# Transposing K with a permutation, so that the score matmuls read runs of 32 columns in place of a stride of 4

## Chip, cores, metric

One core of one Trainium2 chip. The metric is the device time of one execution in microseconds (us). (A run is classed slow when it lies over 1.5% above the fastest of its kernel.) The engines: PE does the matmuls, ACT and DVE the copies, POOL small preparations, SP issues the DMA loads. PSUM is the memory that PE writes to. The granted clock is the share of PE's full clock that the profile shows as allowed.

## The reference, cut

Two independent attention decodes of one token each, A and B, then a concatenation of their outputs.

```python
# for each of A (last 2048 positions) and B (all 8192 positions); Hq = 32 heads, Hkv = 16, Dh = 128
q = (x @ wq).reshape(B, Sq, Hq, Dh)...          # x is 1 x 576
scores = einsum("bhqd,bhkd->bhqk", q, k) * Dh ** -0.5
o = einsum("bhqk,bhkd->bhqd", softmax(scores), v)
out = o.reshape(B, Sq, Hq * Dh) @ wo             # 576 wide
```

There is one query row per head, so almost nothing is computed per byte: 102.9 MB are read in a run, nearly all of it K, V, wq and wo.

## The kernel before

K and V come in slots of 4 MB, two slots each. The work runs in five stages (`g`), each with two K slots. A load into a slot waits until PE has finished reading what lies in it. All big loads go through one queue, in a fixed order.

In a K slot, one 128x128 block holds 32 positions of four heads: partition `4*x + g` holds position `x` of head `g`. PE transposes each block (identity as the moving matrix), ACT and DVE copy the result from PSUM to `kt`, and the score matmuls read `kt` as moving operand, one head at a time:

```python
def k_transpose(c, u, place):            # a unit: a quarter of a slot, 32 blocks
    for q in range(4):
        for t in range(8):
            pe.matmul(ktps_bf[q][:, t*128:(t+1)*128], lhsT=kslots[s][:, o:o+128],
                      rhs=ident[:, :], start=True, stop=True, is_transpose=True)
        # ... ACT (q even) or DVE (q odd) copies the 128 x 1024 bank to kt

def k_scores(c, a, place):               # 16 matmuls for two units
    for g in range(NG):                  # NG = 4 heads
        for j in range(4):               # four column tiles of the array, 32 columns each
            rhs = kt[:, o:o + 2048].rearrange("d (x g) -> d x g", g=NG)[:, :, g]   # stride 4
            pe.matmul(sacc[32*j:32*j+32, 512*h:512*h+512], lhsT=qst[:, o2:o2+32], rhs=rhs, ...)

# order of loads, by stage; k = half a stage's K, v = a V slot, w = wo
order = ["k0 k1 v0", "k2 k3 v1", "k4 k5 v2", "k6 k7 v3", "k8 k9 v4 v5", "w0 v6 v7", "v8 v9 w1 ..."]
# one stage on PE: transposes of units 0..3 (frees slot 0), scores 0, units 4,5, scores 1,
#   units 6,7 (frees slot 1), scores 2, scores 3; after odd stages the softmax transposes; then V slots
```

(Names and offsets shortened, the rest left out.)

## Time and profile before

| | before |
|---|---|
| median of 4 runs | 259.35 us (259.0 to 259.8) |
| profiled run: time, span | 260.13 us, 258.1 us |
| data read, mean rate over the span | 102.9 MB, 399 GB/s |
| PE busy | 185.7 us |
| score matmuls: busy, one | 38.9 us, 628 ns |

Lines of the page of the kernel before. "GB/s" is what DMA moved in each fortieth of the span. A group's line reads: source line, engine, operation, output from inputs, sizes, count, busy us, mean ns of one, idle time before it.

```profile
span 258.1 us, 7455 instructions
...
GB/s 286 446 403 420 427 427 432 422 465 414 422 420 437 434 442 424 361 253 325 366 366 467 427 406 457 437 330 442 432 401 259 406 442 452 406 416 437 426 405 115
...
L481 PE MATMUL ktps<-ident,kv 128*128 128x128 bf16 x1280 | 81.3, 227 | 14.1 <-PEq L214 13.2
...
L506 PE MATMUL sacc<-kt,qst 128*32 128x512 bf16 x320 | 38.9, 628 | 0.0
```

The GB/s row says that DMA is near 430 nearly everywhere, and that it falls to 253 in the eighteenth slice and 259 in the thirty-first. The stretches give the size of those dips. Columns: window, its length, busy time and count of each engine, mean PE clock, DMA share, GB/s (the last number is the one to read).

```profile
103.00:134.00 31.00, 27.71 (x446) 20.87 (x436) 13.15 (x20) 16.47 (x20) 0.80 (x2) 0.93 0.86 342
134.00:160.00 26.00, 22.46 (x300) 15.07 (x301) 14.48 (x22) 15.00 (x17) 0.81 (x2) 1.00 1.01 435
160.00:190.00 30.00, 27.18 (x556) 21.57 (x560) 14.72 (x23) 14.92 (x16) 0.00 (x0) 0.89 0.97 407
190.00:200.00 10.00, 7.57 (x292) 4.97 (x286) 2.92 (x6) 1.26 (x3) 0.00 (x0) 1.00 0.80 319
```

Against the 435 GB/s of 134 to 160 us, the three other stretches lost 31 x (1 - 342/435) = 6.6 us, 1.9 us and 2.7 us of DMA time. Who caused it is in the timeline of the DMA queue (start, duration, what; consecutive issues merged):

```profile
116.27 11.83 SPq L388 DMA_DIRECT2D kv<-in_B_k_cache_dram  x2
128.14 0.60 SPq L388 DMA_DIRECT2D kv<-in_B_v_cache_dram  x1
...
167.39 3.23 SPq L388 DMA_DIRECT2D kv<-in_B_v_cache_dram  x2
...
195.04 27.37 SPq L388 DMA_DIRECT2D kv<-in_B_v_cache_dram  x4
```

The load at 116.27 us is the first K load of the fourth stage; it could not be issued until the last transpose of the slot it overwrites. And PE was late, as the prediction argues, because it spends long on scores. The same timeline for PE; "x4" are the four column tiles of one group, "x16" four groups. The duration is that of the merged records, which overlap, so take the difference of two starts. In brackets, where there was a wait, stand its length and what ended it; PEq is PE's own sequencer, waiting on a semaphore:

```profile
26.17 0.40 PE L439 MATMUL misc<-kv,xpad 128*32 128x512 bf16 x4
26.39 0.40 PE L439 MATMUL opsum<-kv,xpad 128*32 128x512 bf16 x4
...
116.17 1.99 PE L506 MATMUL sacc<-kt,qst 128*32 128x512 bf16 x16
118.09 3.79 PE L481 MATMUL ktps<-ident,kv 128*128 128x128 bf16 x64
```

A group of four q-projection matmuls (128x32 by 128x512, unit stride) starts every 0.215 us. Sixteen score matmuls, the same size, take 118.09 - 116.17 = 1.92 us, 0.45 us for each group of four once 0.1 us for start and end is taken off.

### The profile page before, as it was taken

The numbers are of one execution on the slowest core, as the hardware profiler recorded it, in microseconds if no ns is written. First come the engines' busy times: TensorE is split into PE (matmuls) and PEld (weight loads), VectorE is DVE, ScalarE is ACT, GpSimd is POOL, SyncE is SP. The second block draws the span as 40 slices with busy tenths as digits, with TensorE's granted clock in tenths as the row PEclk, the third lists the DMA queues.
The fourth block names the chain that finished last, engine by engine and source line by source line (L and its number), as shares of the span: only waits on it lengthen the run. The fifth ranks groups of instructions, "written<-read, shape, count | busy, mean of one in ns | idle before, by whom it ended". The sixth has DMA issues, their size and how long they took to land. (4 is left out here: it accounts for less than half of the span.)

```text
span 258.1 us, 7455 instructions
## 1 busy us (share of the span) xinstructions
PE 185.7 (72%) x3371; PEld 134.3 (52%) x3374; DVE 93.6 (36%) x174; ACT 82.8 (32%) x94; POOL 14.5 (6%) x40
## 2 busy tenths in 40 slices
PE   0047539897799967699969995799996551557654
PEld 0013239572777517596648661587755151447642
DVE  0001315544564481165437446245443800230300
ACT  2000017662676500196549550047741000000000
POOL 8801000000000000000000000000000000000000
PEclk9999957999799975799999999599999755556875
DMA  7999999999999999858989999989996999999993
GB/s 286 446 403 420 427 427 432 422 465 414 422 420 437 434 442 424 361 253 325 366 366 467 427 406 457 437 330 442 432 401 259 406 442 452 406 416 437 426 405 115
DMA packets 5355, 102.92 MB, mean 399 GB/s; under 512 B 864, under 2 KB 992, under 8 KB 1376
## 3 DMA queue, kind: packets, MB, share of 16 engines
q1 hardware_dynamic: 5056, 102.77, 94.3%
q8 instruction: 8, 0.13, 0.2%
q10 hardware_dynamic: 288, 0.00, 0.1%
q14 instruction: 3, 0.02, 0.0%
HBM read 102.76 MB, written 0.00 MB: 398 GB/s over the span
## 5 line engine op out<-in xcount | busy, mean ns | idle before, releaser
L489 ACT ACTIVATE kt<-ktps 128x1024 bf16<-128x1024 bf16 x80 | 75.9, 1028 | 71.5 <-PE ktps L481 71.5
L481 PEld LDWEIGHTS ktps<-ident,kv 128*128 128x128 bf16 x1280 | 78.1, 102 | 25.9 <-issue 25.6
L481 PE MATMUL ktps<-ident,kv 128*128 128x128 bf16 x1280 | 81.3, 227 | 14.1 <-PEq L214 13.2
L492 DVE COPY kt<-ktps 128x1024 bf16<-128x1024 bf16 x80 | 55.2, 691 | 48.9 <-PE ktps L481 48.8
L571 PE MATMUL opsum<-kv,ptm 128*32 128x128 bf16 x1280 | 29.4, 273 | 16.5 <-PEq L214 14.7
L506 PE MATMUL sacc<-kt,qst 128*32 128x512 bf16 x320 | 38.9, 628 | 0.0
L571 PEld LDWEIGHTS opsum<-kv,ptm 128*32 128x32 bf16 x1280 | 27.3, 126 | 20.0 <-issue 20.0
L439 PE MATMUL opsum<-kv,xpad 128*32 128x512 bf16 x72 | 8.9, 471 | 17.2 <-DVE xpad L424 17.2
L506 PEld LDWEIGHTS sacc<-kt,qst 128*32 128x32 bf16 x320 | 8.3, 107 | 17.6 <-issue 16.1
L579 DVE TENSOR_SCALAR acc<-opsum,rows 128x128 f32<-128x128 f32 x5 | 1.8, 351 | 41.9 <-PE opsum L571 41.9
L439 PEld LDWEIGHTS opsum<-kv,xpad 128*32 128x32 bf16 x72 | 2.6, 115 | 19.8 <-issue 18.9
L471 POOL COPY qst<-qtm 128x256 bf16<-128x256 bf16 x10 | 4.0, 402 | 140.0 <-PE sacc L506 127.8
L612 ACT ACTIVATE stat<-stat 128x1 f32<-128x1 f32 (+1 forms) x2 | 0.6, 294 | 32.8 <-DVE stat L610 32.8
L655 PE MATMUL ktps<-kv,opj 128*32 128x144 bf16 x200 | 6.7, 296 | 4.0 <-DMA kv<-in_B_wo_dram 3.5
L554 PE MATMUL misc<-pt,spread 128*128 128x512 bf16 x12 | 5.9, 490 | 5.0 <-PEq L214 3.3
L561 DVE TENSOR_TENSOR ptm<-opsum,hmask 128x512 bf16<-128x512 f32 x12 | 8.3, 691 | 1.8 <-PE misc L545 1.8
L445 ACT ACTIVATE qrow<-opsum 128x512 bf16<-128x512 f32 x2 | 1.2, 598 | 24.1 <-PE misc L439 24.1
L439 PE MATMUL misc<-kv,xpad 128*32 128x512 bf16 x72 | 8.8, 464 | 0.0
L561 DVE TENSOR_TENSOR ptm<-misc,hmask 128x512 bf16<-128x512 f32 x12 | 8.2, 686 | 0.5
L532 ACT ACTIVATE psb<-sacc,stat 128x1024 bf16<-128x1024 f32 x3 | 3.3, 1115 | 15.1 <-DVE stat L530 15.1
L655 PEld LDWEIGHTS ktps<-kv,opj 128*32 128x32 bf16 x200 | 4.9, 128 | 5.7 <-DMA kv<-in_B_wo_dram 5.2
L554 PEld LDWEIGHTS opsum<-pt,spread 128*128 128x128 bf16 x12 | 1.2, 98 | 9.6 <-DVE ptm L561 6.6
(67 smaller groups left out, 63.5 us busy)
## 6 DMA issues: line engine op xcount, KB each, us to landing
kv<-in_B_k_cache_dram SPq DMA_DIRECT2D x8, 4096.0 KB
kv<-in_B_v_cache_dram SPq DMA_DIRECT2D x8, 4096.0 KB
kv<-in_A_k_cache_dram SPq DMA_DIRECT2D x4, 2048.0 KB
kv<-in_A_v_cache_dram SPq DMA_DIRECT2D x4, 2048.0 KB
kv<-in_A_wq_dram SPq DMA_DIRECT2D x1, 4608.0 KB, 13.7
kv<-in_A_wo_dram SPq DMA_DIRECT2D x1, 2592.0 KB, 21.0
kv<-in_B_wq_dram SPq DMA_DIRECT2D x1, 2560.0 KB, 19.4
kv<-in_B_wq_dram SPq DMA_DIRECT2D x1, 2048.0 KB, 23.8
```

The lines of the kernel that those rows point to most:

```text
L439: ins = pe.matmul(qps[c][32 * j:32 * j + 32, :], lhsT=xpad[:, P, x, :], rhs=src[:, o:o + 512], start=(u == 0), stop=(u == WQ_UNITS - 1))
L471: add("pool", lambda pool: pool.tensor_copy(qst[:, s * 256:(s + 1) * 256], qtm[:, o:o + 256]), reads=[("qtm", KIND[g])], writes=[("qst", s ...
L481: ins = pe.matmul(ktps_bf[q][:, t * 128:(t + 1) * 128], lhsT=kslots[s][:, o:o + 128], rhs=ident[:, :], start=True, stop=True, is_transpose ...
L489: add("act", lambda act, q=q, dst=dst: act.activation(dst, ktps_bf[q], ACT.Copy), reads=[("bank", q)], writes=[("kt", u % NKT, q)], tag="e ...
L492: add("dve", lambda dve, q=q, dst=dst: dve.tensor_copy(dst, ktps_bf[q]), reads=[("bank", q)], writes=[("kt", u % NKT, q)], tag="e%d%d" % ( ...
L506: ins = pe.matmul(sacc[32 * j:32 * j + 32, 512 * h:512 * h + 512], lhsT=qst[:, o:o + 32], rhs=rhs, start=False, stop=True, skip_group_chec ...
L532: add("act", lambda act: act.activation(psb[:, :], sacc[:, :], ACT.Exp, bias=st(P, C_NB + k), scale=SCALE, accum_out=st(P, C_L + k)), read ...
L554: add("pe", lambda pe, h=h, i=i, dst=dst: pe.matmul(dst[:, :], lhsT=spread[:, i, :], rhs=pt0[:, h * 512:(h + 1) * 512], start=True, stop=T ...
L561: return dve.tensor_tensor(to, dst[:, :].rearrange("p (f n y) -> p f n y", f=4, n=4), m, ALU.mult)
L571: ins = pe.matmul(opsum[32 * j:32 * j + 32, s * DH:(s + 1) * DH], lhsT=ptm[:, o:o + 32], rhs=vslots[s][:, b * 128:(b + 1) * 128], start=(m ...
L579: add("dve", lambda dve: dve.tensor_scalar(acc[:, g, :], opsum[:, 0:DH], rows[:, KIND[g], 0:1], None, ALU.mult), reads=[B_O, "rows"], writ ...
L655: ins = pe.matmul(ktps[P][32 * j:32 * j + 32, 0:OUTW], lhsT=opj[:, P, jj:jj + 32], rhs=view[:, o:o + OUTW], start=(jj == 0), stop=(jj == H ...
```

## The change

The intent: let the transpose, which is a matmul anyway, put the columns into the order that the scores want. Moving a permutation matrix through in place of the identity sends row `4*x + g` to column `32*g + x`. Each head's 32 columns of a block then lie together, and the scores read runs of 32 elements, 256 bytes apart. Number and size of all matmuls and copies stay.

```diff
+    order = nc.alloc_sbuf_tensor("order", [128, 128], BF16)
 ...
-        for t in (ident, xpad, selq, ...):  pool.memset(t[:], 0.0)
+        for t in (ident, order, xpad, selq, ...):  pool.memset(t[:], 0.0)
 ...
+    add("pool", select(order[:].rearrange("p (g x) -> p g x", g=NG), 0, [[-1, NG], [-4, 32]], 1),
+        reads=["order"], writes=["order"])
 ...
-                                    rhs=ident[:, :], start=True, stop=True, is_transpose=True)
+                                    rhs=order[:, :], start=True, stop=True, is_transpose=True)
 ...
-                    rhs = kt[:, o:o + 2048].rearrange("d (x g) -> d x g", g=NG)[:, :, g]
+                    rhs = kt[:, o:o + 2048].rearrange("d (t g x) -> d t g x", g=NG, x=32)[:, :, g, :]
```

(The list of load names is renamed from `order` to `LOADS`, and dependencies name the new tensor.)

More of the change, by code (lines that the diff above doesn't have):

```diff
@@ L356, in setup @@
     def setup(pool):
-        for t in (ident, xpad, selq, warm, qtm, identf, same, pick, spread):
+        for t in (ident, order, xpad, selq, warm, qtm, identf, same, pick, spread):
             pool.memset(t[:], 0.0)
@@ L360, in setup @@
         return pool.memset(opj[:], 0.0)
-    add("pool", setup, writes=["ident", ("xpad", 0), ("xpad", 1), "selq", "ones", "warm", "identf", "pick", "same",
+    add("pool", setup, writes=["ident", "order", ("xpad", 0), ("xpad", 1), "selq", "ones", "warm", "identf", "pick", "same",
                                "spread", ("qtm", 0), ("qtm", 1), ("qtm", 2), ("opj", 0), ("opj", 1)])
@@ L481, in tr @@
                     ins = pe.matmul(ktps_bf[q][:, t * 128:(t + 1) * 128], lhsT=kslots[s][:, o:o + 128],
-                                    rhs=ident[:, :], start=True, stop=True, is_transpose=True)
+                                    rhs=order[:, :], start=True, stop=True, is_transpose=True)
                 return ins
-            add("pe", tr, reads=[("k", s, 0), ("k", s, 1), "ident"], writes=[("bank", q)],
+            add("pe", tr, reads=[("k", s, 0), ("k", s, 1), "order"], writes=[("bank", q)],
                 loop=(c, place + q / 8, K_ON, "inner"))
@@ L704, in bass_concat_heads__sliding_block_cached__gqa_block_cached__decode_kernel @@
     WQ = [("wq", 0, 0), ("wq", 1, 0), ("wq", 1, 5)]
-    order = ["k0 k1 v0", "k2 k3 v1", "k4 k5 v2", "k6 k7 v3", "k8 k9 v4 v5", "w0 v6 v7", "v8 v9 w1 w2 w3 w4 w5 w6 w7"]
+    LOADS = ["k0 k1 v0", "k2 k3 v1", "k4 k5 v2", "k6 k7 v3", "k8 k9 v4 v5", "w0 v6 v7", "v8 v9 w1 w2 w3 w4 w5 w6 w7"]
     def load_more(g):
-        for what in order[g].split():
+        for what in LOADS[g].split():
             i = int(what[1:])
```

## The prediction

> **What bounds the kernel now.** Mostly DMA. The page shows 102.9 MB at a mean of 399 GB/s over a 258.1 us span; in the undisturbed stretch from 134 to 160 us it moves 435 GB/s. At that rate the bytes need 237 us, so 21 are lost: 2.7 in the first 16 us, about 5 after the last weights landed, the rest mostly where the DMA queue ran empty because a load waited for PE to free its slot. Busy time by stretches: 103 to 134 us at 342 GB/s (loses 6.6 us), 160 to 190 at 407 (1.9), 190 to 200 at 319 (2.7). The queue's timeline names the loads: K at 116.27 us (when the fourth transpose unit of stage 2 is done; nothing landed from 114 to 117.5), K at 127.55, V at 167.39, V at 195.04. The chain of waits ends in the wo loads, which only follow in the queue.
>
> **What the change does.** It adds one memset and one select of 128x128 bf16 on POOL (0.2 and 0.3 us for the like ones), which is done at 12.6 us and needed at 24.8. Transposes (1280, 56 ns apart warm) and evictions stay. The scores' moving read changes from stride 4 to runs of 32 elements (64 B), 256 B apart.
>
> In the timeline four column-tiled 128x32 by 128x512 score matmuls take 0.45 us at full clock (630 ns each). The q projection's, same shape, unit stride, take 0.215 us (379 ns each). I take the stride for the cause. The Trainium skill ("TensorE: Matmul & The Clock Gate", Back-to-back issue gap) gives N/2.4 + 2.5 = 216 ns, as the q matmuls show. "SBUF — State Buffer" (Door 1: The DMA port swizzle) says strides up to 8 bf16 are free; the trace disagrees if the stride is the cause (2.1 times at stride 4).
>
> So 16 score matmuls: 1.92 to 0.97 us, 20 times: 19 us less PE time (busy 38.9 to about 20), 3.7 us in each of five stages. Evictions stay hidden: in a transpose run PE (1.83 us a unit) and ACT (1.88) are level, and the last eviction ends 0.8 us after the transposes, just inside the 0.97 us of the third score block.
>
> **How much is on the critical path.** Only what shortens DMA gaps. Walking the queue at 9.75 us per 4.2 MB: stage 1's scores end 3.7 us earlier, hence V slots, stage 2 and the K load of 116.3 too: issued at 112.5, while the queue runs dry at about 113. That gap falls from 4.5 us to about 1. The lead then grows by 3.7 us a stage: the loads of 127.6, 167.4 and 195.0 are issued 0 to 5 us before the queue is empty. About 10 of the 11 us of gaps go; the other 8 or 9 us of PE time become waits for data. Start and tail stay.
>
> **Predicted: 249.8 us, range 247 to 254.** Faster by over 2%: 0.88; within 2%: 0.11; slower: 0.01.
>
> **Right if:** score matmul 380 ns, busy near 20; transposes and evictions unchanged each; no 2 us without DMA between 20 and 250 us; mean rate near 415 GB/s; PE waits longer for K and V; tail as before.
>
> **Wrong if:** runs of 32 still stream slower than a column a cycle, or the score matmuls are slow through their PSUM writes (then no gain); ACT's evictions set the pace (half the gain); a colder PE clock from more idle eats the lead near 107 to 116 us; new gaps appear at V loads.

## The result

252.91 us median of 4 runs (252.21 to 252.96) against 259.35 us. The ratio is 0.9745, 95% interval 0.972 to 0.9769. A ratio is computed as the mean time of one kernel's fast runs over the mean of the other's of the same rounds, so it is not quite the ratio of the medians quoted. On another chip, in the experiments, the same kernel gave 0.9741 (0.9682 to 0.98).

| | before | after |
|---|---|---|
| median | 259.35 us | 252.91 us |
| profiled run: time, span | 260.13, 258.1 us | 252.21, 250.0 us |
| mean DMA rate | 399 GB/s | 412 GB/s |
| PE busy | 185.7 us | 170.4 us |
| score matmuls: busy, one | 38.9 us, 628 ns | 20.7 us, 381 ns |
| K transposes: busy, one | 81.3 us, 227 ns | 82.7 us, 230 ns |
| ACT evictions, one | 1028 ns | 1029 ns |

The page after (line numbers are 4 higher; L510 are the scores):

```profile
span 250.0 us, 7461 instructions
...
GB/s 283 437 390 422 435 425 430 425 454 425 427 417 423 451 430 427 433 410 330 409 409 430 430 425 446 446 425 425 425 415 445 451 435 367 414 416 428 428 402 126
...
L485 PE MATMUL ktps<-order,kv 128*128 128x128 bf16 x1280 | 82.7, 230 | 20.6 <-PEq L214 18.5
...
L510 PE MATMUL sacc<-kt,qst 128*32 128x512 bf16 x320 | 20.7, 381 | 0.0
```

The scores' busy time fell by 18.2 us, and a score matmul (381 ns) now lasts as long as a q matmul at full clock (median 379 ns before). The transposes cost the same with the permutation. The two dips are gone from the GB/s row except for one slice at 330; a shallower one, 367 at 206 to 213 us, is new. The stretches, as before:

```profile
103.00:134.00 31.00, 27.14 (x434) 23.93 (x425) 16.14 (x24) 19.87 (x23) 0.81 (x2) 0.84 0.95 396
...
160.00:190.00 30.00, 26.00 (x723) 22.23 (x712) 13.48 (x21) 16.18 (x18) 0.00 (x0) 0.96 0.99 426
190.00:200.00 10.00, 4.75 (x16) 1.50 (x16) 6.30 (x11) 0.00 (x0) 0.00 (x0) 0.67 1.04 449
```

The losses are now 31 x (1 - 396/435) = 2.8 us, then 0.6 us and nothing (449 is above 435, so -0.3). Together 3.1 us in place of 11.2: 8.1 us gained, as much as the two profiled spans differ by, 258.1 - 250.0. (That the two are equal to the tenth is partly chance: the windows are fixed in time and the work in them moved. Start and tail are within about a microsecond of what they were.) The queue and PE:

```profile
112.52 9.95 SPq L392 DMA_DIRECT2D kv<-in_B_k_cache_dram  x2
122.52 0.60 SPq L392 DMA_DIRECT2D kv<-in_B_v_cache_dram  x1
...
160.48 2.69 SPq L392 DMA_DIRECT2D kv<-in_B_v_cache_dram  x2
...
184.64 30.65 SPq L392 DMA_DIRECT2D kv<-in_B_v_cache_dram  x4
```

```profile
112.42 1.05 PE L510 MATMUL sacc<-kt,qst 128*32 128x512 bf16 x16
113.40 3.79 PE L485 MATMUL ktps<-order,kv 128*128 128x128 bf16 x64
```

The K load is issued at 112.52 us in place of 116.27, the sixteen scores take 0.98 us. Later loads are issued early enough to queue behind others.

PE saved 18 us in its scores and the kernel 6.4. This is no contradiction: what PE saves comes back as waits for data once the queue is never empty. What is left to find out: whether the stride alone was the cause, what in it costs, whether shorter PE time is how the gain came about, and where the 2.8 us went that are still lost.

### The profile page after: what moved, and what is told of

It is laid out like the page before. It is cut to its first block, busy times and chain, and to the rows that moved or that the text cites. A ratio compares the mean times of both kernels' runs of the same rounds, so it can differ in the third digit from the quotient of the medians.

```text
span 250.0 us, 7461 instructions
## 1 busy us (share of the span) xinstructions
PE 170.4 (68%) x3374; PEld 136.0 (54%) x3374; DVE 93.8 (38%) x174; ACT 83.0 (33%) x94; POOL 15.0 (6%) x42
## 5 line engine op out<-in xcount | busy, mean ns | idle before, releaser
L493 ACT ACTIVATE kt<-ktps 128x1024 bf16<-128x1024 bf16 x80 | 76.0, 1029 | 66.0 <-PE ktps L485 66.0
L485 PE MATMUL ktps<-order,kv 128*128 128x128 bf16 x1280 | 82.7, 230 | 20.6 <-PEq L214 18.5
L485 PEld LDWEIGHTS ktps<-order,kv 128*128 128x128 bf16 x1280 | 79.8, 104 | 26.6 <-issue 26.3
L575 PE MATMUL opsum<-kv,ptm 128*32 128x128 bf16 x1280 | 30.2, 277 | 20.2 <-PEq L214 18.1
L575 PEld LDWEIGHTS opsum<-kv,ptm 128*32 128x32 bf16 x1280 | 27.9, 127 | 23.4 <-issue 23.3
L510 PE MATMUL sacc<-kt,qst 128*32 128x512 bf16 x320 | 20.7, 381 | 0.0
L510 PEld LDWEIGHTS sacc<-kt,qst 128*32 128x32 bf16 x320 | 7.0, 96 | 7.9 <-issue 2.1
L558 PE MATMUL opsum<-pt,spread 128*128 128x512 bf16 x12 | 5.4, 454 | 5.5 <-DVE ptm L565 2.8
L659 PE MATMUL ktps<-kv,opj 128*32 128x144 bf16 x200 | 6.1, 291 | 2.2 <-issue 1.1
## 6 DMA issues: line engine op xcount, KB each, us to landing
kv<-in_A_wo_dram SPq DMA_DIRECT2D x1, 2592.0 KB, 20.7
```

The lines of the kernel that those rows point to most:

```text
L485: ins = pe.matmul(ktps_bf[q][:, t * 128:(t + 1) * 128], lhsT=kslots[s][:, o:o + 128], rhs=order[:, :], start=True, stop=True, is_transpose ...
L493: add("act", lambda act, q=q, dst=dst: act.activation(dst, ktps_bf[q], ACT.Copy), reads=[("bank", q)], writes=[("kt", u % NKT, q)], tag="e ...
L510: ins = pe.matmul(sacc[32 * j:32 * j + 32, 512 * h:512 * h + 512], lhsT=qst[:, o:o + 32], rhs=rhs, start=False, stop=True, skip_group_chec ...
L558: add("pe", lambda pe, h=h, i=i, dst=dst: pe.matmul(dst[:, :], lhsT=spread[:, i, :], rhs=pt0[:, h * 512:(h + 1) * 512], start=True, stop=T ...
L575: ins = pe.matmul(opsum[32 * j:32 * j + 32, s * DH:(s + 1) * DH], lhsT=ptm[:, o:o + 32], rhs=vslots[s][:, b * 128:(b + 1) * 128], start=(m ...
L659: ins = pe.matmul(ktps[P][32 * j:32 * j + 32, 0:OUTW], lhsT=opj[:, P, jj:jj + 32], rhs=view[:, o:o + OUTW], start=(jj == 0), stop=(jj == H ...
```

## The experiments

Twelve kernels ran, one of them the changed kernel again. With these inputs the scores are so small that the softmax is close to even, and all five kernels that compute wrong scores passed the comparison with the reference. So a passed comparison does not show the new column order to be right. That rests on the index: row `4*x + g` goes to column `32*g + x`, and a check in arithmetic outside the chip, the transposed block times this matrix read in runs of 32 against the transposed block read with stride 4, found the same numbers for all four heads.

### One half of the change at a time

Identity kept, scores read in runs of 32 (heads get mixed):

```diff
-                                    rhs=order[:, :], start=True, stop=True, is_transpose=True)
+                                    rhs=ident[:, :], start=True, stop=True, is_transpose=True)
```

> Identity kept in the K transposes, scores read runs of 32: wrong result on purpose (heads are mixed). Theory (the moving read's stride of 4 is what cost time): score matmul 379 ns, busy about 20.7 us, time as the changed kernel, 252.9 within 0.8 us. Rival (something of the permutation: another matrix in the transposes, other data in the columns): score matmul 630 ns, time about 259.4.

Permutation kept, scores read with stride 4:

```diff
-                    rhs = kt[:, o:o + 2048].rearrange("d (t g x) -> d t g x", g=NG, x=32)[:, :, g, :]
+                    rhs = kt[:, o:o + 2048].rearrange("d (x g) -> d x g", g=NG)[:, :, g]
```

> Permutation in the K transposes, scores read with stride 4 as before: wrong result on purpose. Theory (stride): score matmul 630 ns, busy about 38.9 us, time as before, 259.4 within 0.8 us. Rival (the permutation): 379 ns and about 253.

Measured on one chip: runs alone 252.03 us, ratio 0.9776 (0.9694 to 0.9858); permutation alone 259.03 us, ratio 1.0015 (0.9941 to 1.009). The score lines of the two, groups by form, runs alone first:

```profile
L510 PE MATMUL sacc<-kt,qst 128*32 128x512 bf16 x320 | 20.7, 382 | 0.0
```

```profile
L510 PE MATMUL sacc<-kt,qst 128*32 128x512 bf16 x320 | 38.8, 628 | 0.0
```

The read pattern makes the whole difference; the permutation costs and gives nothing that these runs can tell (its interval is 0.8% wide to each side). It also settles the rival of the prediction, slow writes to PSUM: both kernels write the same places.

### What in the stride costs

Three other layouts of the same columns, each with a matching permutation where the result stays right: runs of 2 elements 16 bytes apart, stride 2, and (wrong) stride 8.

```diff
# runs of 2
+ select(order[:].rearrange("p (a g y) -> p a g y", g=NG, y=2), 0, [[-8, 16], [-1, NG], [-4, 2]], 1)
+ rhs = kt[:, o:o + 2048].rearrange("d (a g y) -> d a g y", g=NG, y=2)[:, :, g, :]
# stride 2
+ select(order[:].rearrange("p (u x v) -> p u x v", u=2, v=2), 0, [[-2, 2], [-4, 32], [-1, 2]], 1)
+ rhs = kt[:, o:o + 2048].rearrange("d (t u x v) -> d t u x v", u=2, x=32, v=2)[:, :, g // 2, :, g % 2]
# stride 8
+ rhs = kt[:, o:o + 4096].rearrange("d (x g) -> d x g", g=8)[:, :, 2 * g + j % 2]
```

> Correct result. Another permutation: runs of 2 elements (4 bytes), 16 bytes apart. Theory W (a moving read delivers one 4-byte word a cycle, and a bf16 read at stride 4 wastes half a word, nothing else counts): score matmul 379 ns, time about 253. Theory L (the cost is per 16-byte line opened, with two elements of each line used, as with stride 4): 630 ns, time about 259.4.

> Correct result. Another permutation: stride of 2 elements. Theory W (a word of 4 bytes a cycle, one element used of each): 630 ns, time about 259.4. Theory L (16-byte lines, now four elements of each line used): well under 630 ns, 379 if two lines for eight elements hide, time about 253.

> Wrong result on purpose: the scores read with a stride of 8 elements (16 bytes), one element of each line. Theory W: 630 ns, no slower than stride 4, time about 259. Theory L: twice the extra of stride 4 or more, 1000 ns or more for a matmul, and a time of 268 or more. A third view, that only unit stride is fast and all strides cost the same: 630 ns here and at stride 2.

The score lines of the three, in this order:

```profile
L510 PE MATMUL sacc<-kt,qst 128*32 128x512 bf16 x320 | 38.9, 629 | 0.0
```

```profile
L510 PE MATMUL sacc<-kt,qst 128*32 128x512 bf16 x320 | 21.1, 383 | 0.0
```

```profile
L510 PE MATMUL sacc<-kt,qst 128*32 128x512 bf16 x320 | 75.1, 1081 | 0.0
```

Times: runs of 2 259.52 us, ratio 1.0029 (0.9986 to 1.0071); stride 2 252.48 us, ratio 0.9785 (0.9738 to 0.9832); stride 8 291.08 us in one look of unknown state. The word theory (W) is wrong on all three counts, the line theory (L) right on all three: what counts is how many 16-byte lines a matmul touches. A moving read of 512 elements touches, in each partition, 64 lines at unit stride, 128 at stride 2, 256 at stride 4 or in runs of 2, and 512 at stride 8.

Is the cost that of one stream, or do the four column tiles share a port? To see it, lone full-size matmuls with zero weights were put behind each score block, four of each stride:

```diff
+            for i in range(4):   # and the same with strides 4, 8 and 16
+                ins = pe.matmul(sacc[:, 512*h:512*h+512], lhsT=zer[:, :], rhs=v1, start=False, stop=True, ...)
```

> Correct result; only durations count. Each score block is followed by four full-size (not column-tiled) zero-weight matmuls each of stride 1, 4, 8 and 16 elements. Theory S (the four column tiles share one 16-byte line a cycle; a lone stream needs 256 lines for 512 columns at stride 4, 512 at 8 and 16): 379 ns at all four strides. Theory P (each stream pays its own lines, alone or not): 379, about 630, about 1080, about 1080 ns. The four-tile scores themselves stay at 379 ns.

The timeline of PE in this kernel. L511 are the scores, L515, L518, L521 and L524 the lone matmuls of stride 1, 4, 8 and 16; a start to the next start is what four of them take:

```profile
46.69 1.05 PE L511 MATMUL sacc<-kt,qst 128*32 128x512 bf16 x16
47.67 1.04 PE L515 MATMUL sacc<-kt,zer 128*128 128x512 bf16 x4
48.55 1.97 PE L518 MATMUL sacc<-kt,zer 128*128 128x512 bf16 x4
50.34 3.78 PE L521 MATMUL sacc<-kt,zer 128*128 128x512 bf16 x4
53.94 3.85 PE L524 MATMUL sacc<-kt,zer 128*128 128x512 bf16 x4
57.61 6.04 PE L486 MATMUL ktps<-order,kv 128*128 128x128 bf16 x64
```

Theory P holds: four lone matmuls take 0.88 us at stride 1, 1.79 at stride 4, 3.60 at 8 and 3.67 at 16, so 0.22, 0.45, 0.90 and 0.92 us each. Those are the times of a group of four column tiles as well; sharing costs nothing, and a lone stream pays the same. Divided by the lines: 450/256 and 900/512, both 1.76 ns a line. Unit stride and stride 2 (64 and 128 lines, by that figure an estimate of 0.11 and 0.23 us) are under or about level with the 0.215 us that 512 columns take. (Stride 16 costs what stride 8 does and stride 8 twice stride 4: that is what fixes the line at 16 bytes, and not 8 or 32.)

The same trace shows one thing more. Later the granted clock was 0.50 for the unit-stride four and 0.59 on average for the stride-4 four:

```profile
93.39 1.89 PE L515 MATMUL sacc<-kt,zer 128*128 128x512 bf16 x4
95.07 1.99 PE L518 MATMUL sacc<-kt,zer 128*128 128x512 bf16 x4
96.89 3.78 PE L521 MATMUL sacc<-kt,zer 128*128 128x512 bf16 x4
```

Unit stride now takes 1.68 us in place of 0.88, stride 4 takes 1.82 in place of 1.79. (The stride-16 four shown first had run at 0.50 as well.) In this trace the columns slow down with PE's clock and the lines do not. At half clock the two strides cost nearly the same, so a change like this one pays little there. The scores of the changed kernel all ran at full clock: each of their matmuls took 376 to 390 ns.

### Is it PE time that gave the gain?

The first try doubled the score matmuls of the changed kernel, to give PE its old time back with the new reads:

```diff
-            for g in range(NG):
+            for g in [0, 1, 2, 3, 0, 1, 2, 3]:
```

> The changed kernel with every group of score matmuls issued twice (scores doubled, wrong result on purpose): PE's score time is again about 40 us as before the change, but read in runs of 32. Theory (the gain is PE time, which frees slots earlier): time back near 259 (258 to 260.5), score matmul 379 ns, and a stretch without DMA near 114 us is back. Rival (the strided reads cost others time, by taking memory from the evictions or the DMA writes): time stays near 253 to 254.5.

Measured: 268.42 us, ratio 1.0377 (1.0302 to 1.0451), well above what either theory allowed. The score groups did as planned (380 ns each). But the first V slots stalled for no reason that the profile names ("issue", PE waiting for nothing shown); the timeline of PE in this kernel:

```profile
98.01 3.60 PE L575 MATMUL opsum<-kv,ptm 128*32 128x128 bf16 x126 [1.32 <-PEq L214]
104.46 0.23 PE L575 MATMUL opsum<-kv,ptm 128*32 128x128 bf16 x2 [2.86 <-issue]
105.48 3.35 PE L575 MATMUL opsum<-kv,ptm 128*32 128x128 bf16 x123 [0.79 <-PEq L214]
112.73 0.40 PE L575 MATMUL opsum<-kv,ptm 128*32 128x128 bf16 x5 [3.90 <-issue]
```

The two slots took 15 us in place of the changed kernel's 9, and the K load slipped to 123.56 us. So this run could not decide. The stalls come back below. The same test with few instructions:

```diff
+            for i in range(4):                      # four lone matmuls with zero weights per score block
+                o = k0 * UNIT + i * 512
+                ins = pe.matmul(sacc[:, 512*h:512*h+512], lhsT=zer[:, :], rhs=kt[:, o:o + 512], start=False, ...)
```

> Correct result. The changed kernel with four full-size matmuls (128 columns of zero weights, 512 unit-stride columns) added to each score block: 0.87 us of PE time a block, 17 us in all, which is about what the change took away, for 32 PE instructions more in the loop body instead of 128 as in the run that doubled the scores. It redoes that run without its long stalls in the first V pass. Theory (the gain is PE time): 258 to 260 on a chip where before is 258.5 to 259.4. Rival (the strided reads cost others time): 252 to 254.5. Side expectation: the PE stall in the second V slot of the first V pass, after 59 matmuls in the changed kernel, 91 in the run with half the scores, comes after 43, since its place is a place in the instruction stream.

Measured: 260.03 us (257.61 to 261.39), ratio 1.0014 (0.9919 to 1.0109), with the changed kernel at 252.14 us on the same chip. The K load went out at 115.49 us, and the three stretches fell back to 361, 390 and 281 GB/s. So PE time with full-rate reads costs the same, to within about 1%, as PE time with strided reads: the gain is PE time, and strided reads do no other harm that these runs can see.

Then the other direction, half of the scores left out:

```diff
-            for g in range(NG):
+            for g in range(2):
```

> The changed kernel with the scores of two of four heads left out (wrong result on purpose): another 10 us of PE time less, 1.9 us in each stage. Theory (after the change DMA is the limit but for about 2 us lost near 112 to 118 us): time 250.5 to 252.2. Rival (PE still sets the pace in several stages, which would also explain why the change gave 6.5 us and not 9.8): 248 to 250.

Measured: 251.22 us, ratio 0.9702 (0.9629 to 0.9775), about 1 us less than the changed kernel's 0.9741 would give on this chip (0.0039 x 258.5 us); the intervals overlap, and the two ratios come from two chips. PE busy fell by another 10 us, from 170.4 to 160.4, and about a tenth of it reached the time; the intervals would allow up to about a third. PE's speed in the scores is no longer what paces most of the stages.

### Where the last 2.8 us are lost

The half-score run had an oddity: its V slots began 1.4 us earlier than in the changed kernel, and yet its K load went out at 112.71 us, not earlier than 112.52. I thought of the PE clock, which is at half speed in the first V slots (0.50 near 93 to 99 us), and filled PE's waits in the softmax part with dummy matmuls into an idle bank:

```diff
+        def fill(pe, n):
+            for _ in range(n):
+                ins = pe.matmul(ktps[3][:, :], lhsT=ident[:, :], rhs=spread2d, start=True, stop=True)
+            return ins
+        # 3 after the softmax transposes, 1 after each spread matmul, 4 after the last (names shortened)
```

> Correct result. The changed kernel with dummy matmuls into an idle bank while PE waits during the softmax transposes, so that its clock should stay at full in the V slots that follow (0.5 now near 93 to 99 us). Theory (the rest of the gap at the first chunk B K load, about 2 us between 112 and 118 us, is PE lateness): first V slot 2.0 us in place of 3.6, K load issued 1 to 2.5 us earlier, time 0.5 to 2 us below the changed kernel. Rival (the lead is eaten by the stall in the second V slot, whose end does not move): K load within 0.7 us of the old time, no gain.

> The changed kernel again, on the chip of these runs, as their base: 251.5 to 253.3, ratio to before 0.972 to 0.979.

Measured on one chip: 251.9 us with the filling, ratio 0.971 (0.9645 to 0.9775); 252.14 us for the changed kernel, ratio 0.9741 (0.9682 to 0.98). No difference that can be told. The first V pass of the changed kernel on this chip, then of the kernel with the filling, then of the one with half the scores:

```profile
93.93 3.60 PE L575 MATMUL opsum<-kv,ptm 128*32 128x128 bf16 x128 [1.24 <-PEq L214]
97.76 1.79 PE L575 MATMUL opsum<-kv,ptm 128*32 128x128 bf16 x59 [0.22 <-PEq L214]
101.41 1.18 PE L575 MATMUL opsum<-kv,ptm 128*32 128x128 bf16 x69 [1.86 <-issue]
```

```profile
95.07 1.97 PE L583 MATMUL opsum<-kv,ptm 128*32 128x128 bf16 x128 [0.45 <-PEq L214]
97.62 0.83 PE L583 MATMUL opsum<-kv,ptm 128*32 128x128 bf16 x45 [0.58 <-PEq L214]
101.75 1.47 PE L583 MATMUL opsum<-kv,ptm 128*32 128x128 bf16 x83 [3.30 <-issue]
```

```profile
97.82 2.33 PE L575 MATMUL opsum<-kv,ptm 128*32 128x128 bf16 x91 [0.23 <-PEq L214]
102.80 1.01 PE L575 MATMUL opsum<-kv,ptm 128*32 128x128 bf16 x37 [2.65 <-issue]
```

The filling worked as a filling: the first V slot took 1.97 us in place of 3.60. But the second slot stops in the middle, and the stop grew from 1.86 to 3.30 us. What PE gained ahead of it, it waited off there. (K load at 112.39 us with the filling, 112.10 without.) That is what the rival expected.

What stops PE there? Its place moves with the instruction stream. The stop comes after 59 matmuls of the second V slot in the kernel before and in the changed one; after 91 where each pass through the loop has 32 score matmuls less; after 43 where it has 16 matmuls more, as expected beforehand; after 45 with 14 more; and in the kernel with 64 more there are two stops, after 126 matmuls of the first slot and 123 of the second, 125 matmuls apart. Each of these matmuls has a weight load, so 125 are 250 instructions, and the waits between the two slots, which were not counted, come on top. The Trainium skill ("Runtime: NRT & Kernel Launch", Instruction fetch mechanics) says that instructions come in blocks of 16 KiB, 256 instructions, which the sequencer fetches by its own DMA queue, and that the cost of crossing a block is mostly hidden. The places fit blocks of that size, and the stops come only in the first pass through this code (the first pass through the K code has one as well, 1.99 us, ending at 51.37 us in the changed kernel); later V slots take between 1.97 us (full clock) and 3.60 us (half) without one.

The DMA records in the packed traces, which `prof` does not list by time, settle most of the rest. One of the page's two queues named "instruction", q8, moves 16 KiB at a time, in about 1 us. In the changed kernel one such transfer ran from 99.91 to 100.93 us, PE stood still from 100.20 to 102.29, and from 107 to 241 us the queue moved nothing. Each of the eight stops named here, in seven traces, ended 1.36 to 1.58 us after such a transfer had ended. So the stops are waits for instructions, by place, pass and time, and they are not hidden here. No run removed a fetch alone, and why these came late is not shown.

The last run made the V part shorter in time and in instructions, half the V product left out (wrong):

```diff
-            for m in range(32):
+            for m in range(16):
```

> The changed kernel with half the PV matmuls left out of each V slot (wrong result on purpose): 2 to 4 us less PE time before the K load of about 112 us, and half the PE instructions there. Theory (what is left between 103 and 134 us, 2.8 us of DMA time, is that load's lateness, kept late by the PE stall in the second V slot; else DMA is the limit): K load issued at 106 to 110 us, before the queue is empty, that stretch above 425 GB/s, stall gone or under 1 us, time 1.5 to 3 us below the changed kernel, ratio 0.962 to 0.969. Rival (that stretch loses its DMA time to something else, or the lead is spent later): K load early but ratio 0.971 or more.

Measured: 248.95 us (248.87 to 249.02), ratio 0.9571 (0.9545 to 0.9597). Its first V pass, its K load and its stretch:

```profile
94.53 1.90 PE L575 MATMUL opsum<-kv,ptm 128*32 128x128 bf16 x64 [1.24 <-PEq L214]
96.61 1.55 PE L575 MATMUL opsum<-kv,ptm 128*32 128x128 bf16 x64 [0.18 <-PEq L214]
```

```profile
106.16 9.96 SPq L392 DMA_DIRECT2D kv<-in_B_k_cache_dram  x2
```

```profile
103.00:134.00 31.00, 24.06 (x383) 20.83 (x384) 15.89 (x24) 19.91 (x24) 0.80 (x2) 0.89 0.99 427
```

No stop, K load at 106.16 us while older loads were still moving, 427 GB/s where the changed kernel has 396. So the rest of the loss in this stretch was the lateness of that load; 31 x (1 - 427/435) = 0.6 us remain, 2.2 less. How much of the lateness was the stop and how much the V matmuls themselves this run cannot say, since it took away both. The gain is larger than I expected (ratio 0.962 to 0.969, 1.5 to 3 us): by the spans it is 3.2 us (246.8 against 250.0), by the ratios 4.4 us ((0.9741 - 0.9571) x 260.2). The 1 to 2 us beyond the 2.2 were not isolated; this kernel also does half the V work in every later pass and at the end.

No kernel with a right result beat the changed one clearly.

## Why the prediction was right, and where it was off

The range, 247 to 254 us, held the result, and faster by over 2% came true. Point by point:

- Cause. The stride, taken from comparing the score groups with the q groups of the same size, was the cause: each half of the change alone showed it.
- Size of the PE saving. Predicted 38.9 to about 20 us busy and 380 ns; measured 20.7 us and 381 ns. Transposes and evictions did not change, and POOL's two additions (0.21 and 0.32 us) were never waited for.
- Way to the time. Predicted: K load issued at 112.5 us, measured 112.52; the later loads in time; all else becomes waits for data. Adding the PE time back with other matmuls restored the old time, and taking half the scores away gave about 1 us more.
- Size of the gain. Predicted 9.8 us (from 259.61, the median of the three runs then known, to 249.8), measured 6.4. Two terms were mis-sized. First, "about 10 of the 11 us of gaps go": the three stretches regained 8.1 of 11.2 us, and 2.8 of what is left lies at that K load. I had its gap falling to "about 1". The load did go out when predicted, but nearly as the queue ran dry, and from 112 to 118 us DMA moved 283, 279 and 344 GB/s, a loss of 1.8 us against 435. Nor was the lead 3.7 us all the way there: the first V slot began only 2.7 us earlier (95.36 against 98.03 us). The colder clock that the prediction named as a danger goes with that: in the 10 us from 66 us PE's granted clock was 0.71 after and 0.83 before, and the first four transpose units of that stage took 9.8 us in place of 9.0. But it is not why the loss stayed. In the changed kernel's run on the other chip the clock there was 0.86 and the first V slot began at 93.93 us, 4.1 us earlier than before the change; the K load still went out at 112.10 us, and the stretch moved 395 GB/s, as here. Second, I took the gaps from a profiled run and subtracted them from the median. That run was at the slow end of its kernel (260.13 us against a median of 259.35), and the profiled run after at the fast end of its own (252.21 against 252.91): the pair differ by 7.9 us where the medians differ by 6.4. The time of the kernel before varies by more than that: on one chip it ran from 256.19 us at a mean clock of 0.871 to 260.0 at 0.846. Whether the clock is the reason is not shown: on another chip 256.58 and 259.02 us came at the same 0.864.
- "No 2 us without DMA between 20 and 250 us": true up to the tail; from 247 us on, after the last weights, next to nothing moves, as in the kernel before from 255 us on. "Mean rate near 415": 412.

## What to carry to other kernels

When a layout must be gathered and a transpose by matmul is on the way anyway, a permutation matrix does the gathering for nothing, and a matmul's moving read at full clock wants four of a line's eight bf16 elements (four were free here, two were not; three were not tried). Before counting a saving on one engine, walk the queue it feeds: here 18 us of PE time were worth 6.4, out of the 11 us that the DMA queue had lost, and the next 10 us were worth about one. And take the gaps from more than one run, or from a run at the median, before subtracting them from a median.

## What the Trainium skill lacked or had wrong

- "SBUF — State Buffer" (Door 1: The DMA port swizzle) lets bf16 be strided by up to 8 elements for free and asks for two hits on each 16-byte line. For a matmul's moving operand two hits are too few: 0.45 us for 512 columns at stride 4 (two hits) and 0.90 at stride 8, against 0.215 at unit stride; stride 2 (four hits) is free (383 ns a matmul against 381). Runs of two elements per line cost as much as stride 4 (629 ns).
- "TensorE: Matmul & The Clock Gate" (Back-to-back issue gap) has two figures for 512 columns: about 216 ns, which it calls the isolated gap, and about 131 ns for a stream of weight loads and matmuls. The unit-stride groups show the first, 0.215 us, and the lone unit-stride matmuls 0.22 with a weight load each; no run here comes near 131. The SBUF page says that a new line pays a penalty, but no page has its size for a matmul's moving read, 1.76 ns a line (450/256 and 900/512), nor that it does not follow PE's clock (1.82 us for four at stride 4 with the clock at 0.59, 1.79 at full clock), nor that four column tiles at once pay no more for their lines than one matmul alone.
- "Runtime: NRT & Kernel Launch" (Instruction fetch mechanics) calls the crossing of a block of 256 instructions mostly hidden, and warns of a stall only where a taken branch leaves the blocks at hand. In the first pass of a loop, with DMA near full rate, PE stopped for 1.9 to 3.9 us in the middle of straight runs of matmuls, in one run at places 125 matmuls with their weight loads apart, and went on 1.36 to 1.58 us after a 16 KiB instruction transfer had ended. Here the crossings are not hidden.
